# Decoding in place in four slots, separate opening banks, and moved sums in the first two token groups of an attention, gated-layer and expert kernel

## The chip, the cores and the metric

The kernel runs on one core of one Trainium2 chip. The metric is the device time of one execution in microseconds; the median of several runs is given.

## The reference

Three layers follow one another, all in float32. Keys and values are averaged over 8 neighbouring positions, so each of the 8 batches has 72 keys. `w_in` and `w_out` arrive as 64-bit floats.

```python
# q, k, v: (8, 8, 576, 64)
k_p = k.reshape(B, H, 72, 8, D).mean(axis=3);  v_p = likewise
scores = q @ k_p^T / sqrt(D);  attn = softmax(scores);  x = attn @ v_p   # 4608 tokens x 512
h = x @ w_in            # 512 x 2048, float64 in memory
x2 = (h * cos(h)) @ w_out
logits = x2 @ w_gate    # 8 experts, the best one is taken
out = gate_w * (relu(x2 @ w1[e]) @ w2[e])
```

## The kernel before

The 4608 tokens are worked on in 12 groups (g = 0 to 11): 512 tokens, then 256, then 384 each. A group is 16 slots (s = 0 to 15), one for each 128 columns of `w_in`. The order of instructions on every engine is written out by hand; each engine runs its own in that order, and semaphores hold an instruction until what it reads or overwrites is free.

In slot s TensorE (PE) does `mm1(g, s)` into bank HB[s % 2] (L461), then `mm2(g, s - 2)` (L505). The chain between them, in group 0, is: ScalarE (ACT) L479 and L480 (scaled copy and rounded copy), VectorE (DVE) L485, ACT sine L486, DVE product L496, which reads HB[s % 2] and so gives it free for `mm1(s + 2)`, ACT cast L497, GpSimd (POOL) rest L498. L485 reads two tensors in SBUF, L496 one in PSUM.

Group 0 also turns the float64 weights into pairs of float32, in pieces of 128 x 512. Slot s scales the pair of pieces s + 3 on ACT (L600, half before and half behind the sine), does the bit passes of pair s + 2 on DVE, and splits pair s + 1 into high (ACT cast, L612) and low part (POOL, L613), `w_parts`; then `w_load(s + 5)` is issued on SyncE's queue (SP). The bit passes are three for each piece, six a slot: L605 (one tensor in), L606 (two) and L607 (two, the result goes to `u` in SBUF). Their intermediate `b` is a PSUM bank from `rot()`, which in the slots of group 0 hands out banks 5 and 7 in turn:

```python
wl, wh, u, b = self.w[:, :, 0].bitcast(U32), self.w[:, :, 1].bitcast(U32), self.v.bitcast(U32), rot().bitcast(U32)
```

The same two banks take the attention of the next group: `scores(g + 1, i)` (`qk` on PE, L391 to L394, then `soft`: four DVE operations L402, L404 and an exponential L410 on ACT), `norm(i)` (DVE L415 to L417, POOL L418) and `transp(g + 1, i)` (PE L425, copies by ACT L435 and DVE L437). They stand in the list `ex[s]`, which is issued behind the slot's own chain, so on PE they come behind `mm2(s - 2)` and ahead of `mm1(s + 1)`. ACT has the sine in one table and the exponential in another, and loads the table when it changes.

Sums: `pool_k` (L356) and `pool_v` (L378) reduce the keys and values of the next batch on DVE. The raw tiles of batch 1 lie in `kvb`, memory of tags wb8 to wb11, which later holds the converted pieces of `w_out` 8 to 11; so the cast of such a piece waits for the `pool_v` that reads there. Keys are loaded ahead of slot 0, values all four by `early_v` in slot 6.

The opening, ahead of slot 0, does the attention of group 0: four tiles of 128 tokens (`qk`, `soft`, `norm`, `transp`), with runs of `warm` matmuls (L655) between, which give PE something to do. `use(...)` sets the banks that `rot()` hands out, and `warm(n, bank)` writes into the bank named. Then come the bit passes of pairs 0 and 1, `pool_v`, and `pv` (L448 on PE, L452 on ACT, L453 on DVE).

From group 1 on DVE computes the router's logits of the group before, 24 `route_dot` a group (L538, two SBUF tensors in), in numbers for each slot; then `route_sel` (the best expert; L548 to L556) and `route_pos`, which begins with two small matmuls on PE (L569, L570) that read what `route_sel` wrote.

Of the kernel before, what the change touches and what calls it, by code (L numbers as in the profile page):

```python
# [81 lines left out]
def attention_moe_kernel(ctx, tc, qT, kT, vP, w_in, w_out, wg, w1, w2, cst, tri, wgt, out, dbg=None):  # L82
# [25 lines left out]
    def rot():  # L108
        b = rbanks[rot_i[0] % len(rbanks)]
        rot_i[0] += 1  # L110
        return b
# [11 lines left out]
    def w_tmp(s):  # L123
        n_tmp[0] += 1
        return wbp.tile([128, 1024], F32, name=f"tmp{n_tmp[0]}", tag=f"wb{s}")
# [231 lines left out]

    vraw = {}

    def early_v():  # L360
        for c in range(4):
            load_v(1, c)

    def next_k(c):
        if c > 0:
            pool_k(2, c - 1)
# [4 lines left out]
    def load_v(b, c):  # L371
        t = w_tmp(8 + c)[0:KP] if b == 0 else (kvb[c] if b == 1 else raw())[0:KP]
        SP.dma_start(out=t, in_=vP[b, c])
        vraw[b, c] = t
# [8 lines left out]
    def qk(g, i):  # L383
        t0, T = i * TP, BEGIN[g] // TP + i
        b0, b1 = T * TP // S, (T * TP + TP - 1) // S
        sc = [rot(), rot()]
        for pr in range(4):
            for h, r in enumerate((slice(0, 64), slice(64, 128))):
                o = sc[h][:, KP * pr:KP * pr + KP]
                if b0 == b1:  # L390
                    PE.matmul(o, lhsT=qs(g, pr)[r, t0:t0 + TP], rhs=kp[b0 % 2][r, pr], start=True, stop=True)  # L391
                else:
                    PE.matmul(o[0:64], lhsT=qs(g, pr)[r, t0:t0 + 64], rhs=kp[b0 % 2][r, pr], start=True, stop=True)
                    PE.matmul(o[64:128], lhsT=qs(g, pr)[r, t0 + 64:t0 + TP], rhs=kp[b1 % 2][r, pr], start=True, stop=True)  # L394
        return sc
# [74 lines left out]
        DVE.scalar_tensor_tensor(a, r, MAGIC, a, op0=ALU.subtract, op1=ALU.subtract)  # L470
        ACT.activation(a, a, AF.Sin, scale=-TWOPI)  # L471

    def first_slot(s):
        h, a, r = HB[s % 2], tA(0, s % 2), kin[:, 0:W0]
        scales = [p.scale for p in pairs[s + 3]] if s + 3 < NCH else [bool] * 2
        bits = w_bits(s + 2)
        if s > 0:
            w_parts(s + 1)
        ACT.activation(a, h, AF.Identity, scale=INV2PI, bias=consts[:, C_TP + 1:C_TP + 2])  # L479
        ACT.activation(r, a, AF.Identity, bias=consts[:, C_TP + 2:C_TP + 3])  # L480
        if s == 0:
            w_parts(1)
        scales[0]()
        do(bits[0:2])
        DVE.scalar_tensor_tensor(a, r, MAGIC, a, op0=ALU.subtract, op1=ALU.subtract)  # L485
        ACT.activation(a, a, AF.Sin, scale=-TWOPI)  # L486
        scales[1]()
        do(bits[2:4])
        chain_b(0, s)
        do(bits[4:6])  # L490
        w_load(s + 5)

    def chain_b(g, s):
# [93 lines left out]
    class Piece:  # L587
# [11 lines left out]
        def scale(self):  # L599
            ACT.mul(self.w[:, :, 1], self.w[:, :, 1], 2.0 ** -112)  # L600

        def bits(self, u):
            self.v = u
            wl, wh, u, b = self.w[:, :, 0].bitcast(U32), self.w[:, :, 1].bitcast(U32), self.v.bitcast(U32), rot().bitcast(U32)
            return [lambda: DVE.tensor_scalar(b, wh, 3, 0x7FFFFFF8, op0=ALU.logical_shift_left, op1=ALU.bitwise_and),  # L605
                    lambda: DVE.scalar_tensor_tensor(b, wl, 29, b, op0=ALU.logical_shift_right, op1=ALU.bitwise_or),  # L606
                    lambda: DVE.scalar_tensor_tensor(u, wh, 0x80000000, b, op0=ALU.bitwise_and, op1=ALU.bitwise_or)]  # L607
# [30 lines left out]
            for p in pairs[k]:  # L638
                p.scale()

    def w_bits(k):
        if k >= NCH:
            return [bool] * 6
        o = 2 * (k % 3)
        a, b = (p.bits(u) for p, u in zip(pairs[k], us[o:o + 2]))
        return [f for ab in zip(a, b) for f in ab]

    def use(*ids):
        rbanks[:] = [banks[i] for i in ids]
        rot_i[0] = 0  # L650

    def warm(n, bank):

        for i in range(n):
            PE.matmul(banks[bank][:, 384:512], lhsT=ident, rhs=ident, start=True, stop=True)  # L655

    def do(ops):
        for f in ops:
            f()

    def w_parts(k):
        if k < NCH:
            for p in pairs[k]:
                p.parts()
# [23 lines left out]
    u13 = w_tmp(13)  # L688
    us += [u[:, DM * i:DM * i + DM] for u in (u13, ldt[0]) for i in range(2)]
    w_load(2)  # L690
    use(*range(8))
    sc = [qk(0, 0), qk(0, 1)]
    soft(0, sc[0], True)
    pool_v(0, 0)
    soft(1, sc[1], True)
    sc += [qk(0, 2), qk(0, 3)]
    warm(6, 3)
    norm(0, True)
    pool_v(0, 1)
    use(0, 1)  # L700
    transp(0, 0, True)
    warm(4, 7)
    soft(2, sc[2])
    norm(1, True)
    soft(3, sc[3])
    w_scale(0)
    norm(2)
    norm(3)
    use(0, 1)
    bits = w_bits(0)  # L710
    do(bits)
    for i in range(1, 4):
        use(2 * i, 2 * i + 1)
        transp(0, i, True)
        warm((8, 2, 4)[i - 1], (7, 7, 5)[i - 1])
    pool_v(0, 2)
    pool_v(0, 3)
    w_load(3)
    kvb[:] = [w_tmp(8 + i) for i in range(4)]
    for c in range(4):  # L720
        load_k(1, c)
    use(5, 7)
    bits = w_bits(1)
    use(2, 3, 4, 6)
    for c in range(4):
        if c < 2:
            pairs[0][c].parts()
        elif c < 4:
            pairs[1][c - 2].scale()
        pv(0, c)  # L730
        do(bits[0 if c < 2 else c - 2:max(0, c - 1)])
    do(bits[2:6])
    w_load(4)
    w_scale(2)
    ACT.activation(st1[:, 0:1], consts[:, C_TP + 1:C_TP + 2], AF.Sin)
    POOL.tensor_copy(trib, E3[:, 0:256])
    POOL.tensor_copy(run, consts[:, C_OFF:C_OFF + 8])
# [15 lines left out]

    for g in range(NG):
        ex = {s: [] for s in range(NCH)}

        def at(s, f, *a):
            ex[s].append(lambda: f(*a))

        if g + 1 < NG:  # L760
            for i in range(TILES[g + 1]):
                if g == 0:
                    at((6, 10)[i], scores, g + 1, i)
                    at((6, 10)[i], norm, i)
                    at((8, 11)[i], transp, g + 1, i)
                else:
                    o = 1 if g == 1 else 0
                    at(1 + o + 4 * i, scores, g + 1, i)
                    if i == 0 and g > 1:
                        at(1, route_exp)  # L770
                    at(1 + o + 4 * i, norm, i)
                    at(4 + o + 4 * i, transp, g + 1, i)
            if 0 < g < NG - 2:
                at(11 if g == 1 else 10, load_q, g + 2)
            if g == 0:
                at(4, load_q, 1)
                for i in range(2):
                    w = slice(2048 - 2048 * i, 4096 - 2048 * i)
                    at(12 + 2 * i, lambda w=w: SP.dma_start(out=wgb[:, w], in_=wgt[w].unsqueeze(0).to_broadcast([128, 2048])))
                for i in range(3):  # L780
                    at(13 + i, next_k, i)
        dots = {}
        if g > 0:
            last = g == NG - 1
            n = 0
            for s, k in enumerate((0, 3, 4, 3, 4, 3, 4, 3) if last else (0, 2, 1, 3, 3, 2, 1, 3, 3, 2, 1, 3) if g == 1 else (0, 1, 3, 3, 2, 1, 3, 2, 2, 1, 2, 4)):
                dots[s] = list(range(n, n + k))
                n += k
            if last:
                at(1, route_exp)  # L790
                at(8, route_sel, g - 1)
                at(8, route_exp)
                at(9, route_pos)
                at(9, route_gate, g - 1)
                for i in range(3):
                    at(10, route_put, i)
            else:
                at(11 if g == 1 else 12, route_sel, g - 1)
                at(12 if g == 1 else 14, route_pos)
        if g > 1:  # L800
            at(2, route_gate, g - 2)
            for i in range(3):
# [5 lines left out]
                    at((0, 2, 3)[c], load_v, 2, c + 1)  # L808
        for b in range(1, B):
            if g == max(0, b * S // GT - 2):  # L810
                if b == 1:
                    at(6, early_v)
                for c in range(4):
                    if b == 1:
                        at(2 + c, pool_k, b, c)
                        at(7 + c, pool_v, b, c)
                    elif b > 2:
                        at(2 + 2 * c, pool_k, b, c)
                        at(2 * c, load_k, b, c)
                if b == 2:  # L820
                    at(0, next_k, 3)
                    at(1, next_k, 4)
                    at(14, load_v, b, 0)
                if b > 2:
                    for c in range(4):
                        at((7, 10, 12, 14)[c], pool_v, b, c)
                        at((5, 7, 10, 12)[c], load_v, b, c)
        for s in range(NCH):
# [11 lines left out]
                mm2(g, s - 2)  # L840

            if g == 0:
                first_slot(s)
            elif g == NG - 1 and 6 < s < 15:
                c = (s - 7,)
                chain_a(g, s, lambda: split(0, -50, 0, c, False, (0,)))
            else:
                chain_a(g, s)
# [7 lines left out]
            if first_x:  # L856
                E1.append(ep.tile([128, 2048], F32R, name="E1", tag="e1"))
                for i in range(2):
                    tx_parts(XP[i], *unit_x(i))
            todo = dots.get(s, [])  # L860
            if todo:
                route_dot(g - 1, todo.pop(0))
# [363 lines left out]
```

## Time and profile before

| | |
|---|---|
| median of 3 runs | 1481.0 us (1477.67 to 1481.91) |
| profiled execution, own time | 1491.82 us |
| its span | 1490.0 us |
| PE busy | 1423.9 us, 96% of the span |
| DVE / ACT / POOL busy | 878.2 / 735.6 / 448.4 us |
| granted PE clock, mean | 0.983 |

The profiled execution is longer than the median by 10.8 us. Busy time is a sum over the whole span; what holds PE up in a certain slot is read from the waits and the timeline there. A clock of 1.00 is 2.4 GHz, 0.50 is 1.2 GHz.

### The profile page before, as it was taken

To read this page: it belongs to the slowest core of one execution; us is meant where nothing else is said; L and a number is where in the kernel's file an instruction comes from. 1 tells how busy PE (TensorE), PEld (TensorE's weight loads), DVE (VectorE), ACT (ScalarE), POOL (GpSimd) and SP (SyncE) were. 2 spreads that over 40 slices of the span, in tenths; PEclk is the share of its full clock that TensorE was granted. 3 is DMA by queue.
4 is the path that set the end of the run, shared out by engine and by line. 5 is a ranking of instruction groups with operands and counts; after the bars stand their busy time and mean duration, and the time that the engine had idled before them with its cause. 6 is when DMAs were issued, how large, how long until landed. Compare 5 with 4: busy or idle time off the path is not lost. (4 is left out here: it accounts for less than half of the span.)

```text
span 1490.0 us, 23426 instructions
## 1 busy us (share of the span) xinstructions
PE 1423.9 (96%) x8343; PEld 1224.6 (82%) x8343; DVE 878.2 (59%) x1948; ACT 735.6 (49%) x1360; POOL 448.4 (30%) x421
## 2 busy tenths in 40 slices
PE   7878989999999999999999999999999999999998
PEld 5656778888898988888888888888787878899997
DVE  6976677867686867586867585863252142124222
ACT  5866566566565656565656565661131131123111
POOL 2654223233333333232324242432131121113212
PEclk9988999999999999999999999999999999999999
DMA  7552202200121200121200001215565434001110
GB/s 245 189 162 104 67 30 69 62 23 22 40 64 42 62 30 22 37 63 38 69 31 22 22 1 43 94 37 203 212 236 195 151 146 153 31 29 55 50 37 31
DMA packets 42485, 119.96 MB, mean 81 GB/s; under 512 B 6227, under 2 KB 21715, under 8 KB 39520
## 3 DMA queue, kind: packets, MB, share of 16 engines
q1 hardware_dynamic: 34416, 99.17, 19.7%
q0 software_dynamic: 7920, 18.97, 4.0%
q8 instruction: 73, 1.20, 0.3%
q14 instruction: 76, 0.62, 0.2%
HBM read 101.55 MB, written 19.66 MB: 81 GB/s over the span
## 5 line engine op out<-in xcount | busy, mean ns | idle before, releaser
L505 PE MATMUL bank<-wb,GB 128*128 128x512 f32 x1696 | 434.0, 396 | 0.1
L461 PE MATMUL bank<-xh,WI 128*128 128x384 f32 (+2 forms) x1504 | 427.9, 347 | 5.7 <-DVE att L496 3.5
L505 PEld LDWEIGHTS bank<-wb,GB 128*128 128x128 f32 x1696 | 315.2, 188 | 71.1 <-issue 5.3
L461 PEld LDWEIGHTS bank<-xh,WI 128*128 128x128 f32 x1504 | 278.7, 192 | 22.0 <-DVE att L496 4.2
L461 PE MATMUL bank<-xl,WI 128*128 128x384 f32 (+2 forms) x752 | 256.7, 341 | 0.0
L937 PEld LDWEIGHTS bank<-E,wb 128*128 128x128 f32 x1632 | 210.8, 192 | 20.3 <-issue 8.7
L937 PE MATMUL bank<-E,wb 128*128 128x256 f32 x1632 | 216.6, 285 | 4.2 <-DVEq L1142 2.1
L538 DVE SCALAR_TENSOR_TENSOR E<-x2t,wgb 128x512 bf16<-128x512 f32 x264 | 213.1, 807 | 2.1
L946 PE MATMUL bank<-wb,xh 128*128 128x512 f32 x816 | 210.4, 396 | 0.0
L928 ACT ACTIVATE xh<-bank 128x256 fp32r<-128x256 f32 x136 | 52.2, 384 | 297.8 <-PE bank L937 296.1
L929 DVE SCALAR_TENSOR_TENSOR xh<-bank,xh 128x256 fp32r<-128x256 f32 x136 | 57.6, 424 | 218.0 <-ACT xh L928 91.9
L498 POOL TENSOR_TENSOR GB<-E,GB 128x384 fp32r<-128x384 f32 (+1 forms) x88 | 96.4, 1095 | 243.7 <-ACT GB L497 207.7
L498 POOL TENSOR_TENSOR GB<-TA,GB 128x384 fp32r<-128x384 f32 (+1 forms) x88 | 97.7, 1110 | 234.8 <-ACT GB L497 234.8
L946 PEld LDWEIGHTS bank<-wb,xh 128*128 128x128 f32 x816 | 145.5, 189 | 25.4 <-issue 0.2
L461 PEld LDWEIGHTS bank<-xl,WI 128*128 128x128 f32 x752 | 144.4, 192 | 6.5
L199 POOL DMA_INDIRECT E<-x2d,E x44 | 46.0, 1045 | 271.5 <-PE bank L744 258.2
L470 DVE SCALAR_TENSOR_TENSOR TA<-bank,TA 128x384 f32<-128x384 f32 (+1 forms) x88 | 47.4, 539 | 77.0 <-ACT bank L468 75.7
L470 DVE SCALAR_TENSOR_TENSOR E<-bank,E 128x384 f32<-128x384 f32 (+1 forms) x88 | 47.5, 540 | 59.9 <-ACT bank L468 58.8
L497 ACT CAST GB<-E 128x384 fp32r<-128x384 f32 (+2 forms) x96 | 49.3, 513 | 65.4 <-DVE E L496 61.9
L471 ACT ACTIVATE E<-E 128x384 f32<-128x384 f32 (+1 forms) x88 | 45.4, 516 | 68.5 <-DVE E L470 68.3
L467 ACT ACTIVATE TA<-bank,consts 128x384 f32<-128x384 f32 (+1 forms) x88 | 49.6, 564 | 44.4 <-PE bank L461 44.4
L497 ACT CAST GB<-TA 128x384 fp32r<-128x384 f32 (+1 forms) x88 | 44.5, 505 | 53.8 <-DVE TA L496 46.5
(243 smaller groups left out, 1747.9 us busy)
## 6 DMA issues: line engine op xcount, KB each, us to landing
rst<-w SPq DMA_DIRECT2D x12, 2048.0 KB
stg<-w SPq DMA_DIRECT2D x6, 2048.0 KB
x2d<-x2t SPq DMA_DIRECT2D x36, 256.0 KB
QF<-qT SPq DMA_DIRECT2D x10, 768.0 KB
E<-kT SPq DMA_DIRECT2D x24, 288.0 KB
E<-vP SPq DMA_DIRECT2D x24, 288.0 KB
wgb<-w_in SPq DMA_DIRECT2D x11, 512.0 KB
wgb<-w_out SPq DMA_DIRECT2D x11, 512.0 KB
```

The costliest lines, as they stand in the source:

```text
L199: POOL.indirect_dma_start(out=xg[i], out_offset=None, in_=x2d[0:n], in_offset=bass.IndirectOffsetOnAxis(ap=column(u, i)[0], axis=0), bound ...
L461: PE.matmul(o, lhsT=a, rhs=xT(g, k, c), start=n == 0, stop=n == 11)
L467: ACT.activation(a, h, AF.Identity, scale=INV2PI, bias=consts[:, C_TP + 1:C_TP + 2])
L470: DVE.scalar_tensor_tensor(a, r, MAGIC, a, op0=ALU.subtract, op1=ALU.subtract)
L497: ACT.copy(h, a)
L498: POOL.tensor_tensor(l, a, h.bitcast(F32), op=ALU.subtract)
L505: PE.matmul(acc, lhsT=a[:, sl], rhs=w_tile(s)[:, DM * w:DM * w + DM], start=s == 0 and n == 0, stop=s == NCH - 1 and n == 2)
L538: DVE.scalar_tensor_tensor(junk, x2[i], 1.0, wgb[:, DM * e:DM * e + DM], op0=ALU.mult, op1=ALU.mult, accum_out=lgs[:, i, e:e + 1])
L928: ACT.activation(h, o, AF.Relu)
L929: DVE.scalar_tensor_tensor(l, o, 0.0, h.bitcast(F32), op0=ALU.max, op1=ALU.subtract)
L937: PE.matmul(o, lhsT=w_tile(4 * w + s // 2)[:, f], rhs=x[:, c], start=n == 0, stop=n == 11)
L946: PE.matmul(OP[i], lhsT=a[s % 3][:, 128 * i:128 * i + 128], rhs=w_piece(w, s), start=s == 0 and n == 0, stop=s == 7 and n == 2)
```

## The change

The bit passes of slots 6, 8, 9 and 11 use `u` itself for the intermediate, so they take no PSUM bank, and all their operands lie in SBUF. The scores of the second tile move from slot 10 to slot 9. `norm` moves one slot later and stands ahead of L485 (a new list `soon`). Values are loaded one by one behind each `pool_k`, one slot earlier, and `pool_v` goes to slots 5, 7, 8 and 10. In slot 0 the order within the chain changes, and the two scale passes `w_scale(2)` come there from the opening. In the opening the `warm` matmuls get bank 7 for themselves and the other uses other banks. In group 1, dots, `norm`, one key sum, `route_sel` and `route_pos` move to other slots.

```diff
-    def first_slot(s):
+    def first_slot(s, soon):
         h, a, r = HB[s % 2], tA(0, s % 2), kin[:, 0:W0]
-        bits = w_bits(s + 2)
+        bits = w_bits(s + 2, s in (6, 8, 9, 11))
         if s > 0:
             w_parts(s + 1)
         ACT.activation(a, h, AF.Identity, scale=INV2PI, bias=consts[:, C_TP + 1:C_TP + 2])
         ACT.activation(r, a, AF.Identity, bias=consts[:, C_TP + 2:C_TP + 3])
         if s == 0:
+            w_scale(2)
             w_parts(1)
+        else:
+            do(bits[0:2])
         scales[0]()
-        do(bits[0:2])
+        for f in soon:
+            f()
         DVE.scalar_tensor_tensor(a, r, MAGIC, a, op0=ALU.subtract, op1=ALU.subtract)
         ACT.activation(a, a, AF.Sin, scale=-TWOPI)
         scales[1]()
-        do(bits[2:4])
+        do(bits[0:2] if s == 0 else bits[2:4])
         chain_b(0, s)
-        do(bits[4:6])
+        do(bits[2:6] if s == 0 else bits[4:6])
         w_load(s + 5)
...
-        def bits(self, u):
+        def bits(self, u, place):
...
+            b = u if place else rot().bitcast(U32)
...
-    def warm(n, bank):
+    def warm(n):
...
-            PE.matmul(banks[bank][:, 384:512], lhsT=ident, rhs=ident, start=True, stop=True)
+            PE.matmul(banks[7][:, 0:128], lhsT=ident, rhs=ident, start=True, stop=True)
...
-    use(*range(8))
+    use(0, 1, 2, 3, 4, 5)
...
-    sc += [qk(0, 2), qk(0, 3)]
-    warm(6, 3)
+    sc.append(qk(0, 2))
+    warm(4)
+    use(6, 0)
+    sc.append(qk(0, 3))
     norm(0, True)
     pool_v(0, 1)
-    use(0, 1)
+    use(1, 3)
     transp(0, 0, True)
-    warm(4, 7)
+    warm(4)
...
-    use(0, 1)
+    use(2, 3)
     bits = w_bits(0)
     do(bits)
-    for i in range(1, 4):
-        use(2 * i, 2 * i + 1)
-        transp(0, i, True)
-        warm((8, 2, 4)[i - 1], (7, 7, 5)[i - 1])
+    for i, two in enumerate(((1, 4), (5, 1), (6, 0))):
+        use(*two)
+        transp(0, i + 1, True)
+        warm((8, 2, 4)[i])
...
+    kvb_i[0] = -1
...
-    use(5, 7)
+    use(2, 3)
     bits = w_bits(1)
-    use(2, 3, 4, 6)
+    use(4, 5, 1, 6)
...
-    w_scale(2)
...
-                    at((6, 10)[i], scores, g + 1, i)
-                    at((6, 10)[i], norm, i)
+                    at((6, 9)[i], scores, g + 1, i)
+                    soon[(7, 10)[i]].append(lambda i=i: norm(i))
                     at((8, 11)[i], transp, g + 1, i)
...
-                    at(1 + o + 4 * i, norm, i)
+                    if g == 1:
+                        soon[3 + 4 * i].append(lambda i=i: norm(i))
+                    else:
+                        at(1 + 4 * i, norm, i)
...
-                at(4, load_q, 1)
+                at(1, load_q, 1)
...
-  (0, 2, 1, 3, 3, 2, 1, 3, 3, 2, 1, 3) if g == 1
+  (2, 3, 1, 2, 3, 3, 1, 2, 3, 2, 0, 2) if g == 1
...
-                at(11 if g == 1 else 12, route_sel, g - 1)
-                at(12 if g == 1 else 14, route_pos)
+                at(12, route_sel, g - 1)
+                at(14, route_pos)
...
-                if b == 1:
-                    at(6, early_v)
                 for c in range(4):
                     if b == 1:
-                        at(2 + c, pool_k, b, c)
-                        at(7 + c, pool_v, b, c)
+                        at(1 + c, pool_k, b, c)
+                        at(1 + c, load_v, b, c)
+                        at((5, 7, 8, 10)[c], pool_v, b, c)
...
-                    at(1, next_k, 4)
+                    at(3, next_k, 4)
```

## Rows read from the trace of the kernel before

**Rows 1.** Windows: busy us (x instructions) of each engine, PE clock, DMA share, GB/s.

```profile
275.00:1490.00 1215.00, 1188.17 (x7060) 1030.37 (x7059) 673.98 (x1540) 561.99 (x1034) 339.65 (x325) 0.99 0.21 71
```

**Rows 2.** Waits of PE, whole span: us in total, times, longest.

```profile
PE bank L425 <- DVE tmp L607: 6.9, 2, 4.1
PE bank L393 <- DVE E L607: 6.2, 1, 6.2
PE bank L569 <- DVE oh L556: 5.1, 2, 4.2
PE bank L461 <- DVE att L496: 3.5, 1, 3.5
PE bank L391 <- ACT GB L497: 3.4, 1, 3.4
```

**Rows 3.** Windows behind two of these waits, columns as in rows 1.

```profile
80.00:82.00 2.00, 1.91 (x33) 1.55 (x34) 0.87 (x2) 1.23 (x1) 1.27 (x1) 0.50 0.42 120
211.00:216.00 5.00, 4.89 (x24) 4.50 (x24) 1.93 (x9) 2.13 (x5) 0.75 (x1) 0.66 0.00 0
```

**Rows 4.** Timeline of the opening: start, us, engine, instruction, [idle before <-releaser].

```profile
18.72 1.15 POOL L418 TENSOR_TENSOR tmp<-tmp,rss 128x576 f32<-128x576 f32 x1 [1.96 <-DVE rss L417]
...
23.80 0.46 DVE L402 TENSOR_REDUCE mxs<-bank 128x4 f32<-128x288 f32 x1 [4.41 <-PE bank L655]
24.80 2.05 PE L655 MATMUL bank<-consts 128*128 128x128 f32 x16 [0.17 <-DVE tmp L404]
...
28.75 1.07 PE L425 MATMUL bank<-consts,tmp 128*72 128x128 f32 x8
...
34.37 0.51 PE L461 MATMUL bank<-xh,WI 128*128 128x512 f32 x1
```

**Rows 5.** Timeline of DVE, from the product of slot 3 to that of slot 4.

```profile
61.34 0.68 DVE L496 TENSOR_TENSOR E<-bank,E 128x512 f32<-128x512 f32 x1
61.94 1.27 DVE L607 SCALAR_TENSOR_TENSOR E<-tmp,bank 128x512 uint32<-128x512 uint32 x2
...
65.24 0.72 DVE L485 SCALAR_TENSOR_TENSOR att<-E,att 128x512 f32<-128x512 f32 x1 [0.18 <-ACT E L480]
65.89 1.28 DVE L606 SCALAR_TENSOR_TENSOR bank<-wgb,bank 128x512 uint32<-128x512 uint32 x2
67.08 0.68 DVE L496 TENSOR_TENSOR att<-bank,att 128x512 f32<-128x512 f32 x1
```

**Rows 6.** Timeline of DVE and POOL, slots 1 and 4.

```profile
46.91 1.84 DVE L485 SCALAR_TENSOR_TENSOR E<-E,E 128x512 f32<-128x512 f32 x1 [0.89 <-issue]
46.92 1.29 POOL L613 TENSOR_TENSOR wb<-E,wb 128x512 fp32r<-128x512 f32 x1
...
65.37 1.76 POOL L613 TENSOR_TENSOR wb<-E,wb 128x512 fp32r<-128x512 f32 x1
```

**Rows 7.** Timeline of DVE and ACT, slots 6 and 7.

```profile
81.53 0.46 DVE L402 TENSOR_REDUCE mxs<-bank 128x4 f32<-128x288 f32 x1 [1.12 <-PE bank L394]
83.37 0.68 ACT L410 ACTIVATE tmp<-tmp 128x576 f32<-128x576 f32 x1 [2.14 <-DVE tmp L404]
84.09 0.75 DVE L415 TENSOR_REDUCE rss<-tmp 128x8 f32<-128x576 f32 x1 [0.75 <-ACT tmp L410]
...
86.22 0.69 ACT L479 ACTIVATE E<-bank,consts 128x512 f32<-128x512 f32 x1 [1.14 <-PE bank L461]
88.25 1.28 ACT L486 ACT_TABLE_LOAD   x1
...
92.01 1.21 DVE L378 TENSOR_REDUCE E<-tmp 72x128 f32<-72x1024 f32 x1
```

**Rows 8.** Timeline of ACT, start of slot 8.

```profile
93.26 0.62 ACT L612 CAST wb<-x2t 128x512 fp32r<-128x512 f32 x1 [1.10 <-DVE E L378]
```

**Rows 9.** Timeline of PE, first matmuls of slots 13 and 14.

```profile
136.84 0.39 PE L461 MATMUL bank<-xh,WI 128*128 128x512 f32 x1
...
142.43 0.39 PE L461 MATMUL bank<-xh,WI 128*128 128x512 f32 x1
```

More of the change, by code (lines that the diff above doesn't have):

```diff
@@ L358, in attention_moe_kernel @@
     vraw = {}
-    def early_v():
-        for c in range(4):
-            load_v(1, c)
     def next_k(c):
@@ L600, in scale @@
             ACT.mul(self.w[:, :, 1], self.w[:, :, 1], 2.0 ** -112)
-        def bits(self, u):
+        def bits(self, u, place):
             self.v = u
-            wl, wh, u, b = self.w[:, :, 0].bitcast(U32), self.w[:, :, 1].bitcast(U32), self.v.bitcast(U32), rot().bitcast(U32)
+            wl, wh, u = self.w[:, :, 0].bitcast(U32), self.w[:, :, 1].bitcast(U32), self.v.bitcast(U32)
+            b = u if place else rot().bitcast(U32)
             return [lambda: DVE.tensor_scalar(b, wh, 3, 0x7FFFFFF8, op0=ALU.logical_shift_left, op1=ALU.bitwise_and),
@@ L639, in w_scale, with w_bits @@
                 p.scale()
-    def w_bits(k):
+    def w_bits(k, place=False):
         if k >= NCH:
@@ L644, in w_bits @@
         o = 2 * (k % 3)
-        a, b = (p.bits(u) for p, u in zip(pairs[k], us[o:o + 2]))
+        a, b = (p.bits(u, place) for p, u in zip(pairs[k], us[o:o + 2]))
         return [f for ab in zip(a, b) for f in ab]
@@ L727, in attention_moe_kernel @@
             pairs[0][c].parts()
-        elif c < 4:
+        else:
             pairs[1][c - 2].scale()
@@ L755, in attention_moe_kernel @@
         ex = {s: [] for s in range(NCH)}
+        soon = {s: [] for s in range(NCH)}
         def at(s, f, *a):
@@ L770, in attention_moe_kernel @@
                         at(1, route_exp)
-                    at(1 + o + 4 * i, norm, i)
+                    if g == 1:
+                        soon[3 + 4 * i].append(lambda i=i: norm(i))
+                    else:
+                        at(1 + 4 * i, norm, i)
                     at(4 + o + 4 * i, transp, g + 1, i)
@@ L785, in attention_moe_kernel @@
             n = 0
-            for s, k in enumerate((0, 3, 4, 3, 4, 3, 4, 3) if last else (0, 2, 1, 3, 3, 2, 1, 3, 3, 2, 1, 3) if g == 1 else (0, 1, 3, 3, 2, 1, 3, 2, 2, 1, 2, 4)):
+            for s, k in enumerate((0, 3, 4, 3, 4, 3, 4, 3) if last else (2, 3, 1, 2, 3, 3, 1, 2, 3, 2, 0, 2) if g == 1 else (0, 1, 3, 3, 2, 1, 3, 2, 2, 1, 2, 4)):
                 dots[s] = list(range(n, n + k))
@@ L842, in attention_moe_kernel @@
             if g == 0:
-                first_slot(s)
+                first_slot(s, soon[s])
             elif g == NG - 1 and 6 < s < 15:
@@ L859, in attention_moe_kernel @@
                     tx_parts(XP[i], *unit_x(i))
+            if g == 1:
+                for f in soon[s]:
+                    f()
             todo = dots.get(s, [])
```

## The prediction

> **What bounds the kernel now.** I read the waits of PE first, then the windows, then the timeline of each engine around the longest waits. From 275 us to the end PE is busy 1188 of 1215 us at a clock of 0.99 [rows 1]. The change touches nothing there, so what is won or lost ahead of 275 us reaches the end one to one. Ahead of it the reader is to see five kinds of wait [rows 2]: PE waits 6.9 us in two pieces and 6.2 us in one for L607, the last bit pass of a slot; 3.4 us at the scores of slot 10, where the view names ACT but the banks were held by bit passes too; 3.5 us for L496 of slot 0; and 4.2 us in one piece for `route_sel`. All but the 3.5 and the 4.2 come from one thing: scores and transposes take their banks from the same two as the bit passes of the slot just issued, and PE, in order, stands until DVE has done that slot. Behind such a wait the clock was 0.50 for a stretch (80 to 82) and 0.66 over 211 to 216 [rows 3], so each costs more than its own length: 5 us at 0.66 are 1.7 us lost.
>
> Between attention slots DVE and ACT set the pace. From L496 of slot 3 to that of slot 4 are 5.74 us [rows 5]. L485 starts 3.3 us behind the end of L496 (61.94, where the next pass starts) and waited only 0.18 us for ACT; then come 0.65 for L485, 1.2 for two L606 and 0.6 for L496. PE needs 5.6 us for a slot (136.84 to 142.43) [rows 9], so such slots keep it nearly full, and every addition on that chain makes PE wait.
>
> **The opening.** DVE stands 4.41 us ahead of the second half of tile 3's scores, until `warm` matmuls in the same bank are done [rows 4]. With bank 7 for `warm` alone this wait goes, and the first transposes no longer stand behind 12 matmuls that themselves wait for a bank. What is late next? The `norm` of tile 1 on POOL ends at 18.72 + 1.15 = 19.87 whatever the banks do; the transposes of tile 1 take 1.07 (as those at 28.75) and end at 20.95. From the matmuls behind them (24.80) to the first `mm1` (34.37) PE took 9.57 us, of which some 0.1 was waiting for things that are now early. The same list of work follows now, so `mm1(0)` starts at 20.95 + 9.45 = 30.4: **4.0 us earlier**. DVE's bit passes move by more than that (its 4.41 us are gone ahead of them), so PE is the later of the two. Bounds: nothing, if the first weights land only just in time, which no row shows; 4.4 us, all of DVE's wait.
>
> Slot 0: L485 no longer follows two bit passes, but its sine now stands on ACT behind two scale passes more. The one takes off about what the other adds, so I count the 3.5 us wait as it is, and its bounds are nothing gained and 1 us gained. At the product of slot 5 the lead is still 4.0: between slots 1 and 5 the chain of 5.74 us rules, and the key sums, moved one slot earlier, lie beside it as they do now: in slot 4 DVE had such a sum and still waited 0.18 us for ACT [rows 5]. The moved loads of values and queries stand on SP's queue behind `w_load` of their slot, with nothing behind them but the `w_load` of the next, a slot later.
>
> **Slots 6 to 12.** I follow L496 to L496. A slot on DVE is: two L607 (1.2), what `ex` adds, two L605 (1.2), L485 (0.65), two L606 (1.2), L496 (0.6) [rows 5].
>
> *The four slots in place.* L606 and L607 get a second SBUF operand, and L605 its output in SBUF; the trace before has no such pass. The nearest row is L485, also with two SBUF operands: 0.72 us against 0.64 for a pass with PSUM, with the same 0.65 from start to start [rows 5]. I take the same length. But rows 6 show a price: L485 of slot 1 took 1.84 us, and its POOL neighbour, which started 0.01 us later, the usual 1.29; in slot 4 L485 was there first, and the POOL operation took 1.76. DVE and POOL pass each other one whole operation at a time when DVE reads two SBUF tensors. The Trainium skill has this in SBUF — State Buffer, section Who interferes with whom: a VectorE instruction with two SBUF inputs and a GpSimd instruction that reads SBUF shut each other out for a whole instruction; it speaks against the change, and the rows agree. The page VectorE: DVE Perf Modes, section Mode 2×_2P, adds that a single-input operation within SBUF may go at two results a cycle, so L605 in place could be some 0.3 us shorter each, an estimate that no row here bears out.
>
> POOL has three operations a slot. The third is due at 65.37, 3.4 us behind the end of L496, and lasts 1.29, so it ends 4.7 us behind it [rows 5, 6]. DVE comes to L485 at 1.2 + 1.2 (`pool_v` [rows 7]) + 1.2 = 3.6, while POOL is at work. I let POOL keep its turn once: L485 at 4.7, the passes behind it free, and the period is 4.7 + 0.65 + 1.2 + 0.6 = 7.15 for slots 6, 8 and 11. Slot 9 has a copy of 0.6 more on DVE, which pushes POOL a little too: 7.4. If DVE never loses, L485 starts at 3.6 (4.2 in slot 9): 6.05 and 6.65, together 4.1 us less. If two more POOL operations go first in every one of the four, 4 x 2 x 1.29 = 10.3 us more.
>
> *The two slots behind scores (7 and 10).* From the end of L496: 1.2 for L607, 1.84 for the four DVE operations of the softmax (81.53 to 83.37), then ACT's chain: from the exponential to L479 1.71 us (86.22 less its wait of 1.14 for PE, less 83.37), to the table 2.03, the table 1.28; then 0.66 for the sine and 0.6 for L496 [rows 7]: 9.35 us. `norm` now stands inside that chain ahead of L485, where DVE waits for ACT anyway: it is due 1.2 behind the softmax, after the L605 pair, and done about 1.1 later (84.09 with its 0.75 and two short ones), while ACT gives L485 free 1.71 + 1.4 behind the exponential. If the cover were gone it would cost 1.1 us twice.
>
> *Slot 12* has a copy of 0.6 and ACT another: 6.2. The second cast of slots 8, 9 and 10, which waited for `pool_v` (1.10 in slot 8 [rows 8]), no longer does, since its `pool_v` is now a slot or more earlier; slot 11 still does, hidden behind POOL's third operation.
>
> Sum: 3 x 7.15 + 7.4 + 2 x 9.35 + 6.2 = 53.75 us from L496 of slot 5 to that of slot 12. `mm1(14)` starts 0.65 us behind it: 54.4. Before, L496 of slot 5 was at 67.08 + 5.74 = 72.8, and `mm1(14)` at 142.43 [rows 5, 9]: 69.6. **Gain 15.2 us.** PE fits in: its seven slots need 7 x 5.6 = 39.2, the transposes 1.07 twice [rows 4], and the scores an estimated 2 twice, from their sixteen small matmuls: some 45. It still waits, but the scores of slot 6 wait for the passes of slot 5 only (some 1 us against 6.2), and the transposes of slots 8 and 11 for those of 7 and 10 (some 3 us each against 4.1 and 2.8). Those of slot 11 may leave the clock low for one `mm1`; that stands close to the end of the chain, and I take off **1.3 us** for it (bounds 0 and 2.6: from nothing to 24 matmuls at the lower level, half of it hidden).
>
> **Group 1.** With `route_sel` in slot 12 and `route_pos` two slots behind it, PE's matmuls come when DVE has long been done: the 4.2 us go, and the 1.7 us of low clock [rows 2, 3]. Dots in slot 0 stand ahead of L496 there and read rows that ACT has just copied; I charge 0.6 us for them, and with 24 dots as before nothing else. The key sum that moves from slot 1 to 3 only leaves more time for its load. **Gain 5.3 us.**
>
> **Sum.** 4.0 + 15.2 - 1.3 + 5.3 = 23.2 us. The profiled execution's 1491.8 becomes 1468.6; the median of the runs is 10.8 below the profiled one, and I take the gain from it whole: 1481.0 - 23.2 = **1457.8**.
>
> **The rivals.**
>
> *POOL goes first.* In the four slots DVE loses two more turns: 10.3 us less gain, 1468. For it: in slot 1 POOL's next operation went ahead of a DVE instruction that came at the same moment [rows 6]. Against: POOL has only three operations a slot, and two have mostly run by the time the in-place pairs come.
>
> *The opening gives nothing.* The first weights or their scaling are what is late next: 1481.0 - 19.2 = 1462. For it: no row shows when they land. Against: DVE's passes there waited for nothing once the 4.41 us were over.
>
> *Attention waits as before.* The banks are still held, by the slot before, and DVE is later in it; if each of the four places waits as long as before, only opening and group 1 are left, 9.3 us, and something of slots 8 to 10: 1470. For it: slots 7 and 10 stay at 9.35 us, so L607 there comes late. Against: the chain above.
>
> *Slower: the clock stays low.* PE would be busy some 45 of 54 us in slots 6 to 12. If it were at 0.50 throughout, a slot would need nearly twice its 5.6 us, some 10.5, which is 2.8 more than the mean period of 7.7: 20 us over seven slots, and 4.9 for each slot behind. It decides from slot 13 on, where the 23 us are used up; up to the end of slot 15 it comes to some 34 us: 1492. Against: in rows 3 the level of 0.50 ended while PE worked on, and 211 to 216 was mixed, with 4.9 of 5 us busy.
>
> **How the numbers follow.** The sum has 0.62; POOL first 0.15; no gain in the opening 0.11; attention waits as before 0.07; low clock 0.04; and 0.01 is left for no change. A measurement here can tell some 0.3%, or 4.4 us. So faster 0.95, same 0.01, slower 0.04. The likeliest case alone reaches from 1452 (DVE never loses, no low clock) to 1463. For 8 in 10 the range takes in the first two rivals: 1451 to 1469.
>
> **What would show it.** `mm1(0)` near 30.4; L402 of tile 3 without a wait; the scores of slot 6 waiting about 1 us; L485 in slots 6, 8, 9 and 11 up to 1.7 us long; L496 of slots 7 and 10 some 9.3 us behind the one before; `mm1(14)` near 123; no wait at L569 in group 1. It is wrong if in-place passes are themselves longer than 0.7 us, if they queue behind POOL one by one, or if `mm1` runs at half speed through whole slots.

## The result, and the profile after

The changed kernel takes 1461.0 us (median of 4 runs, 1459.35 to 1462.11) and the kernel before, beside it, 1480.6 (1477.67 to 1481.91): a ratio of 0.987, with a 95% interval of 0.985 to 0.989. That is 19.6 us less. Forecast were 1457.8 us, 23.2 less, with a range of 1451 to 1469.

The two profiled executions stand further apart than that: spans of 1490.0 and 1457.5, or 32.5 us. So I compare by place: the first matmul, the first `mm1` of slot 14, the first scores in group 1 and the first in group 2 stood at 34.37, 142.43 [rows 4, 9], 169.51 and 232.46 before. The timeline of PE shows the last two before, and then all four after, with the transposes of slot 11 among them:

```profile
169.51 1.43 PE L391 MATMUL bank<-E,QF 64*128 64x72 f32 x16 [1.95 <-DMA QF<-qT]
...
232.46 1.11 PE L391 MATMUL bank<-E,QF 64*128 64x72 f32 x16
```

```profile
30.77 0.50 PE L457 MATMUL bank<-xh,WI 128*128 128x512 f32 x1
...
112.41 1.89 PE L421 MATMUL bank<-consts,tmp 128*72 128x128 f32 x8 [3.92 <-DVE x2t L608]
...
126.87 0.39 PE L457 MATMUL bank<-xh,WI 128*128 128x512 f32 x1
...
155.36 0.89 PE L387 MATMUL bank<-E,QF 64*128 64x72 f32 x12 [2.13 <-DMA QF<-qT]
...
212.57 1.11 PE L387 MATMUL bank<-E,QF 64*128 64x72 f32 x16
```

The lead grows from 3.6 to 15.6, sinks to 14.2 and is 19.9 in group 2. All of the measured 19.6 us is there. The other 12.6 us of the span difference arise behind it, in the expert layer, which the change does not touch. Two rows by line, of before and then of after, show from when to when one group of six small matmuls ran, and what they waited for in all:

```profile
L1022 PE MATMUL bank<-consts,xl x6: 273/421/476, 1054.3 to 1212.1; 128*128 128x128 f32 x6
its engine sat idle before it (us, times) until:
  ACT xl L1019: 8.0, 3
```

```profile
L1031 PE MATMUL bank<-consts,xl x6: 272/300/328, 1032.5 to 1181.4; 128*128 128x128 f32 x6
its engine sat idle before it (us, times) until:
  ACT xl L1028: 1.5, 3
```

Before it took 157.8 us, after 148.9: 8.9 of the 12.6. The rest lies in two pieces of some 1.9 us, ahead of these matmuls and behind them. The wait of three times 2.7 us in place of 0.5 goes with the chip and not with the kernel (last section). The 10.8 us by which the profiled execution of before stood above the other runs are of the same size; that they have this cause is likely, and not shown.

The waits of PE, longest first, without those of the expert layer, answer to [rows 2]:

```profile
PE bank L421 <- DVE x2t L608: 8.0, 2, 4.1
...
PE bank L457 <- DVE att L496: 2.7, 1, 2.7
...
PE bank L389 <- DVE tmp L608: 0.8, 2, 0.5
```

The 6.2 us at the scores of slot 6 are down to 0.8 in two pieces, the 3.4 at the scores of slot 10 and the 4.2 for `route_sel` are gone. The transposes, L421, still wait 8.0 us: some 3 us each were forecast, and 4.07 and 3.92 came. The windows show that the rest is as full as it was [rows 1], and the clock behind the second of these waits:

```profile
255.11:1457.50 1202.39, 1181.28 (x7060) 1027.68 (x7059) 675.93 (x1540) 562.07 (x1034) 339.46 (x325) 1.00 0.21 72
...
113.00:116.00 3.00, 3.00 (x12) 2.47 (x11) 1.66 (x3) 1.94 (x4) 3.00 (x3) 0.50 0.82 295
116.00:118.70 2.70, 2.70 (x10) 2.12 (x9) 2.68 (x3) 1.62 (x3) 1.04 (x1) 0.70 0.17 67
```

What the forecast got wrong in size is in the timeline of DVE and POOL in slot 6, from the product of slot 5 to that of slot 6 (start, us, instruction; beside [rows 5, 6]):

```profile
69.05 0.68 DVE L496 TENSOR_TENSOR E<-bank,E 128x512 f32<-128x512 f32 x1
69.65 1.27 DVE L608 SCALAR_TENSOR_TENSOR tmp<-wgb,bank 128x512 uint32<-128x512 uint32 x2
70.84 1.20 DVE L374 TENSOR_REDUCE E<-tmp 72x128 f32<-72x1024 f32 x1
71.97 0.74 DVE L606 TENSOR_SCALAR E<-tmp 128x512 uint32<-128x512 uint32 x2
72.95 1.47 DVE L485 SCALAR_TENSOR_TENSOR att<-E,att 128x512 f32<-128x512 f32 x1 [0.23 <-ACT E L476]
74.35 2.39 DVE L607 SCALAR_TENSOR_TENSOR E<-tmp,E 128x512 uint32<-128x512 uint32 x2
76.66 0.68 DVE L496 TENSOR_TENSOR att<-bank,att 128x512 f32<-128x512 f32 x1
...
71.81 2.06 POOL L614 TENSOR_TENSOR WI<-tmp,WI 128x512 fp32r<-128x512 f32 x1
73.84 1.75 POOL L614 TENSOR_TENSOR wb<-tmp,wb 128x512 fp32r<-128x512 f32 x1
```

From 71.97 on the two engines take turns. DVE's L606 pair runs until 72.71, and POOL's first L614, which has its usual 1.28 us to do, takes 2.06. DVE's L485 starts at 72.95 and ends at 74.42, 0.55 behind that POOL operation. POOL's second L614 then ends at 75.59, and DVE's L607 pair, 1.28 us of work, ends 1.15 behind that. The period is 7.61 us; 7.15 were forecast. Not every pass takes turns: the sum, L374, with one input in SBUF, ran its usual 1.20 us while POOL's L498, from 70.58 on, ran its usual 1.28.

L485 and the L607 pair have two inputs in SBUF. For them this is the rule named ahead of the result (the Trainium skill, SBUF — State Buffer, section Who interferes with whom), and the trace agrees with it for two turns in a row, not for one. The L606 pair has only one input, and POOL still lost 0.78 us beside it. In place that pair took 0.74 us, where a pair with PSUM takes 1.28. The Trainium skill, VectorE: DVE Perf Modes, section Mode 2×_2P, has two results a cycle for one input within SBUF; the prediction's estimate from it was some 0.3 us less for each pass, and the trace agrees, with some 0.27 less.

### The profile page after: what moved, and what is told of

Its sections match the earlier page's. It is cut to its first block, busy times and chain, and to the rows that moved or that the text cites. A ratio compares the mean times of both kernels' runs of the same rounds, so it can differ in the third digit from the quotient of the medians.

```text
span 1457.5 us, 23415 instructions
## 1 busy us (share of the span) xinstructions
PE 1410.9 (97%) x8339; PEld 1214.8 (83%) x8339; DVE 884.8 (61%) x1948; ACT 734.5 (50%) x1360; POOL 454.0 (31%) x421
## 5 line engine op out<-in xcount | busy, mean ns | idle before, releaser
L457 PEld LDWEIGHTS bank<-xh,WI 128*128 128x128 f32 x1504 | 275.3, 189 | 22.7 <-DVE E L496 5.3
L498 POOL TENSOR_TENSOR GB<-E,GB 128x384 fp32r<-128x384 f32 (+1 forms) x88 | 96.5, 1097 | 236.7 <-ACT GB L497 201.6
L498 POOL TENSOR_TENSOR GB<-TA,GB 128x384 fp32r<-128x384 f32 (+1 forms) x88 | 97.4, 1107 | 229.5 <-ACT GB L497 229.5
```

Source lines behind the costliest of these rows:

```text
L457: PE.matmul(o, lhsT=a, rhs=xT(g, k, c), start=n == 0, stop=n == 11)
L498: POOL.tensor_tensor(l, a, h.bitcast(F32), op=ALU.subtract)
```

## The experiments

Times were compared with the kernel before on the same chip. On three further chips that kernel took 1488.8, 1479.1 and 1489.6 us, so only differences are used. A second run of the changed kernel tells how far a single trace can be trusted:

> The changed kernel once more, as the measure for the two others on the same chip: 19.6 us under the kernel before by every theory, within the scatter of a few us.

It took 1473.0 us against 1489.6, a ratio of 0.990 (0.988 to 0.991): 16.6 us less. From the first `mm1` to the scores in group 2 it took 183.9 us, where the first execution took 181.8 (212.57 less 30.77) and the kernel before 198.1. I call this stretch "the way to group 2". Two traces of one kernel differ by 2 us in it, so less than that is not told apart below.

Of these 2 us 1.2 are a single turn, in slot 2, whose period was 5.71 us in the first execution and 6.88 in the second. L485 and a POOL operation start 0.02 us apart there; in the first execution DVE had the turn, in the second POOL:

```profile
49.96 0.69 DVE L485 SCALAR_TENSOR_TENSOR att<-E,att 128x512 f32<-128x512 f32 x1 [0.17 <-ACT E L476]
49.98 1.84 POOL L614 TENSOR_TENSOR wb<-x2t,wb 128x512 fp32r<-128x512 f32 x1
```

```profile
50.08 1.86 DVE L485 SCALAR_TENSOR_TENSOR att<-E,att 128x512 f32<-128x512 f32 x1 [0.18 <-ACT E L476]
50.10 1.30 POOL L614 TENSOR_TENSOR wb<-x2t,wb 128x512 fp32r<-128x512 f32 x1
```

So where the two come within some 0.02 us of each other, one and the same kernel goes either way, and a forecast turn by turn is open there by one turn.

**The opening alone** (bank 7 for `warm`, the other banks dealt out anew and the scores of tile 3 behind the first `warm` matmuls, in the kernel before):

```diff
...
-            PE.matmul(banks[bank][:, 384:512], lhsT=ident, rhs=ident, start=True, stop=True)
+            PE.matmul(banks[7][:, 0:128], lhsT=ident, rhs=ident, start=True, stop=True)
...
-    use(2, 3, 4, 6)
+    use(4, 5, 1, 6)
```

> The kernel before with the opening's banks alone changed (warm matmuls in a bank of their own, other uses apart); slots and group 1 as before. Theory (the wait for the warm matmuls' bank held up the whole opening): the first matmul of slot 0 starts near 30.8 in place of 34.4, and the time is 3 to 4 us under the kernel before, about 1477 us. Rival (the later stalls of group 0 swallow the lead, because VectorE's chain and not PE sets them): the lead is gone by slot 14, and the time is within 1 us of 1480.6.

1477.0 against 1479.1, a ratio of 0.9988 (0.9977 to 0.9999): 2.1 us less. The first `mm1` is at 30.60, 3.8 us earlier, and the product of slot 5 still 3.6 earlier (69.26 against 72.84). By slot 12 the lead is 2.3 (135.19 against 137.52): slots 7, 9 and 11 took 0.8, 0.1 and 0.3 us longer than before. In slot 7 the loss is PE's: the low clock behind the scores of slot 6 lasted longer. From 3.0 to 4.8 us behind the start of that slot's matmuls the clock was still 0.50, where it was 0.94 in the kernel before (second row), and ACT waited 1.92 us for them in place of 1.14:

```profile
81.06:82.86 1.80, 1.80 (x5) 1.37 (x5) 1.73 (x5) 0.46 (x1) 0.99 (x1) 0.50 0.76 193
...
84.62:86.42 1.80, 1.80 (x8) 1.41 (x8) 1.73 (x5) 0.66 (x2) 0.99 (x1) 0.94 0.77 187
```

So by itself the opening keeps about half of what it gains at its own place, between theory and rival; the interval takes in 0.1 to 3.4 us.

**In place undone:**

```diff
-        bits = w_bits(s + 2, s in (6, 8, 9, 11))
+        bits = w_bits(s + 2, False)
```

> The changed kernel with the bit passes of all slots in PSUM again; everything else stays changed. Theory (in-place passes free the banks): scores of slots 6 and 9 and transposes of slots 8 and 11 wait on PE for the last bit pass of their own slot again, 3 to 6 us each; the first matmul of slot 14 comes some 11 us later than in the changed kernel (126.9), and the time is about 1472 us. Rival (the port shared with GpSimd takes back what the free banks give, and the gain of the slots came from the moved sums and norm): within 2 us of 1461.

1480.2 against 1488.8, 0.994 (0.991 to 0.997): 8.6 us less than before, where the whole change brought 16.6 to 19.6. The way to group 2 is 192.0 us, 8 to 10 longer than in the changed kernel. From the first `mm1` to that of slot 14 it is 106.2 us, 9 to 10 longer (96.1 and 97.2), where some 11 were expected; the rival is out. The wait of the scores of slot 6 is back among the waits of PE:

```profile
PE bank L421 <- DVE tmp L608: 7.1, 2, 4.1
PE bank L389 <- DVE E L608: 6.4, 1, 6.4
```

That of the transposes (L421) was there in the changed kernel too, 8.0 us against 7.1 here: this wait is not what the change takes away. Slots 7, 9, 10 and 12 took 2.1 to 2.9 us longer without the in-place passes, and slots 6, 8 and 11 0.8 to 1.7 us less, which is what in-place passes cost there.

**Group 1 as before** (its dots, `norm`, `route_sel`, `route_pos` and one key sum where they were):

```diff
...
-                at(12, route_sel, g - 1)
+                at(11 if g == 1 else 12, route_sel, g - 1)
...
-                    at(3, next_k, 4)
+                    at(1, next_k, 4)
```

> The changed kernel with the dots, norm, key sum, best-expert step and its matmuls of group 1 in their old slots. Theory (what was won in group 1 is one wait of PE for the best-expert step and the low clock behind it): that wait of about 4 us is back, and the time is 5 to 6 us more, about 1466.5 us. Rival (VectorE is as full either way, so the wait only moves to another place in group 1 or 2): within 2 us of 1461.

1476.5 against 1488.8, 0.991 (0.989 to 0.993): 12.3 us less, so these moves are worth 4 to 7. The wait is back whole, and the way to group 2 is 188.8 us, 5 to 7 longer:

```profile
PE bank L569 <- DVE oh L556: 5.0, 2, 4.2
```

**In place in slots 2 to 5 as well**, where no attention needs a bank:

```diff
-        bits = w_bits(s + 2, s in (6, 8, 9, 11))
+        bits = w_bits(s + 2, s in (2, 3, 4, 5, 6, 8, 9, 11))
```

> The changed kernel with slots 2 to 5 in place as well, where no attention stands that could gain by it. Theory (an in-place slot costs the turns that VectorE and GpSimd take at the shared port): each of the four goes from 5.75 us to about 7.6, so the product of slot 5 comes some 7.5 us later than at 69.05, and the time is about 1468.5 us. Rival (slots 6, 8, 9 and 11 are long because of the sums and copies in them, not because of the port): under 1 us a slot, so 1461 to 1464 us.

1477.8 against 1488.8, 0.993 (0.991 to 0.995): 11.0 us less, so 6 to 9 slower than the changed kernel. The four slots took 30.0 us in place of 23.0 (products at 45.80 and 75.81; 46.05 and 69.05 in the changed kernel). This is what in-place passes cost where they save no wait. In slots 3 to 5 a period was 7.6 us, the same as in slots 6 and 8. DVE again takes its turns behind POOL:

```profile
55.51 2.30 DVE L606 TENSOR_SCALAR E<-tmp 128x512 uint32<-128x512 uint32 x2
57.73 1.77 DVE L485 SCALAR_TENSOR_TENSOR E<-E,E 128x512 f32<-128x512 f32 x1
```

**POOL reads nothing beside the in-place passes.** The low parts of the weights in these four slots are filled with zeros, so this part of the computation is left out.

```diff
...
+            if blank:
+                POOL.memset(lo.bitcast(F32), 0.0)
+            else:
+                POOL.tensor_tensor(lo, v, hi.bitcast(F32), op=ALU.subtract)
...
```

> The changed kernel, but in slots 6, 8, 9 and 11 GpSimd writes zeros for the low parts of the weights in place of subtracting; so the low parts of weight pairs 7, 9, 10 and 12 are left out of the result. Theory (turns at the shared port): the rounding subtraction and the second bit pass of these slots run at 0.7 us each without standing behind GpSimd, the four slots shrink from 7.6 to 8.2 us to about 6.0 to 6.6, and the time is 4 to 6 us less than the changed kernel, 1455 to 1457 us. Rival (in-place passes are slow by themselves, or ScalarE's chain sets these slots): within 1.5 us of 1461.

1466.3 against 1488.8, 0.986 (0.984 to 0.987): 22.5 us less. The periods of slots 6, 8, 9 and 11 are 6.08, 6.09, 6.31 and 6.85 us; the first two are the 6.05 that the prediction gave for a DVE that never loses. That is close in part by luck, since its L606 pair was counted at 1.2 us and took 1.43, as slot 6 shows:

```profile
72.13 1.43 DVE L606 TENSOR_SCALAR E<-tmp 128x512 uint32<-128x512 uint32 x2
73.47 0.68 DVE L485 SCALAR_TENSOR_TENSOR att<-E,att 128x512 f32<-128x512 f32 x1
74.08 1.28 DVE L607 SCALAR_TENSOR_TENSOR E<-tmp,E 128x512 uint32<-128x512 uint32 x2
```

POOL's two writes, 0.53 us each, are over by 72.95, and L485 and the L607 pair, alone then, have their usual length. The L606 pair has not: beside the writes it took 1.43 and not 0.74, so the fast pass within SBUF was held up by operations of POOL that read nothing. So the run shows what the two turns behind POOL's subtractions cost together: at least 1.5 us in slots 6 and 8 (7.61 less 6.08).

**The second low part later.** Computed in full, but POOL's second subtraction of these four slots is issued behind the product:

```diff
+        later = []
+        if s in (6, 8, 9, 11):
+            pairs[s + 1][0].parts()
+            pairs[s + 1][1].parts(later)
...
         chain_b(0, s)
+        do(later)
...
```

> The changed kernel, but in slots 6, 8, 9 and 11 the second low part of the weights is subtracted by GpSimd behind the slot's own rest, one operation later, when the in-place passes ahead of the product are over. Theory (in these slots the shared port is full: VectorE's operations on it and GpSimd's three add up to the whole slot): slots 6 and 8 shrink from 7.6 us by about 1, slot 9 stays, slot 11 shrinks a little, and the time is 1.5 to 3 us under the changed kernel. Rival (order on GpSimd changes nothing, its operations come one slot later at the same cost): within 1 us of the changed kernel.

1467.7 against 1489.6, 0.986 (0.984 to 0.987): 21.9 us less, and 5.3 us under the changed kernel on this chip (1473.0), whose range of runs it does not touch (1466.8 to 1468.5 against 1471.5 to 1477.3). That is more than the 1.5 to 3 us expected. Slots 6 and 8 took 6.50 us and slot 11 6.85, together 3.1 us less; what the other 2 us are is open. Slot 6 shows that only the first turn is left:

```profile
73.32 0.75 DVE L611 TENSOR_SCALAR E<-tmp 128x512 uint32<-128x512 uint32 x2
74.30 1.47 DVE L489 SCALAR_TENSOR_TENSOR att<-E,att 128x512 f32<-128x512 f32 x1 [0.23 <-ACT E L480]
75.69 1.28 DVE L612 SCALAR_TENSOR_TENSOR E<-tmp,E 128x512 uint32<-128x512 uint32 x2
...
73.16 2.07 POOL L619 TENSOR_TENSOR WI<-tmp,WI 128x512 fp32r<-128x512 f32 x1
...
79.89 1.30 POOL L619 TENSOR_TENSOR wb<-tmp,wb 128x512 fp32r<-128x512 f32 x1
```

Slot 9 kept 8.21 us, and it supports the same reading. The operation put off from slot 8 lies in it, so POOL has two subtractions there as before, and the L612 pair still loses its turn:

```profile
95.63 2.43 POOL L619 TENSOR_TENSOR wb<-x2t,wb 128x512 fp32r<-128x512 f32 x1
98.02 1.74 POOL L619 TENSOR_TENSOR WI<-tmp,WI 128x512 fp32r<-128x512 f32 x1
98.53 2.38 DVE L612 SCALAR_TENSOR_TENSOR E<-tmp,E 128x512 uint32<-128x512 uint32 x2
```

**In place in slots 7 and 10 too**, so that the transposes of slots 8 and 11 need no bank of theirs:

```diff
-        bits = w_bits(s + 2, s in (6, 8, 9, 11))
+        bits = w_bits(s + 2, 5 < s < 12)
```

> The changed kernel with slots 7 and 10 in place as well, so that the transposes of slots 8 and 11 need no bank of theirs. Theory (VectorE's chain sets slots 6 to 12, and PE's two waits of 4 us at the transposes only show it): the waits shrink to about 2.5 us, where norm is due, but the two slots get longer by up to 1.5 us each at the shared port; the time is the same or up to 3 us more, 1461 to 1464 us. Rival (these waits of PE cost their length): 3 to 4 us less, about 1457.5 us.

1463.5 against 1479.1, 0.989 (0.987 to 0.992): 15.5 us less, no better than the changed kernel, and some 3 us short of two runs on the same chip that are not told from it (18.6 and 18.3, below). The wait for L608 is gone, and another stands in its place, for `norm` on POOL:

```profile
PE bank L421 <- POOL tmp L414: 3.2, 2, 2.4
```

The scores of slot 9 also wait 2.92 us now, for a copy on ACT (0.17 in the changed kernel, for one on DVE). Slots 7 and 10 took 10.06 and 10.15 us, 0.8 to 0.9 more. So the 8.0 us at the transposes are no price of the banks: PE is ahead of the softmax and waits for it in one form or another.

**Three moves undone, one at a time:** `norm` back in slots 6 and 9; the sums of the values and their loads back where they were; slot 0 in its old order.

```diff
-                    soon[(7, 10)[i]].append(lambda i=i: norm(i))
+                    at((6, 9)[i], norm, i)
```

> The changed kernel with norm of group 0 directly behind its scores, in slots 6 and 9, as it stood before. Theory (one slot later it lies in time in which VectorE waits for ScalarE): VectorE then waits for the exponential with the bit passes of the next slot queued behind norm; 0.5 to 1.5 us more for each, so 1462 to 1464 us. Rival (it costs nothing either way): within 1 us of 1461.

```diff
-                        at(1 + c, load_v, b, c)
-                        at((5, 7, 8, 10)[c], pool_v, b, c)
+                        at(6, load_v, b, c)
+                        at(7 + c, pool_v, b, c)
```

> The changed kernel with the four loads of values in slot 6 and their sums in slots 7 to 10, as before. Theory (the second weight cast of slots 8, 9 and 10 stands on ScalarE until the sum has read the memory that it writes): ScalarE waits 1.1 us in each of these slots again, of which a part lies on the chain; 1 to 3 us more, 1462 to 1464 us. Rival (these slots are set by VectorE and the port, so ScalarE has room): within 1 us of 1461.

```diff
...
-        do(bits[0:2] if s == 0 else bits[2:4])
+        do(bits[2:4])
         chain_b(0, s)
-        do(bits[2:6] if s == 0 else bits[4:6])
+        do(bits[4:6])
...
```

> The changed kernel with the order of slot 0 as before and the two scale passes back in the opening. Theory (what slot 0 wins it gives back in slot 1, where the four bit passes that it pushed behind the product make the next casts late): the product of slot 0 comes some 0.8 us later, those of slots 2 to 5 within 0.4 us, and the time is within 1 us of the changed kernel. Rival (the chain's lead in slot 0 stays): 1 us more or above.

They took 18.6, 18.3 and 18.2 us less than before, with ratios of 0.988 (0.985 to 0.990), 0.988 (0.986 to 0.990) and 0.988 (0.986 to 0.989). The way to group 2 was 183.3, 184.3 and 183.0 us. None is told from the changed kernel: each of the three moves is worth less than some 2.5 us here, alone. The traces say more of the first two: the periods of slots 6 to 12 add up to 56.95 and 57.11 us there and to 56.97 in the changed kernel, so in these slots `norm` and the values gain nothing. The 1 to 3 us more that the theory expected of each did not come.

## Why the prediction was right, and where its sizes were off

The mechanism held: in-place passes free the banks, the opening and group 1 lose their waits, and POOL takes part of the gain back. The sizes did not all hold. By place, the lead is 3.8 us at the product of slot 5, another 11.8 up to `mm1` of slot 14, 1.4 lost up to the scores of group 1, and 5.7 in group 1: 19.9. The forecast was 4.0, 13.9 (15.2 less 1.3), nothing and 5.3.

**The opening** came as forecast: `mm1(0)` at 30.77 for 30.4, and the second half of tile 3's scores is no longer waited for. What was late next was PE's own list of work, not the first weights. That the time fits so well is partly luck. The matmuls behind the transposes of tile 1 were to start at 20.95 and start at 22.22, since PE was still busy with `warm` matmuls when `norm` was done. From there the list took 8.55 us and not 9.45. Of the 9.57 before, 0.1 was taken for waiting; one wait for `norm` on POOL (L418) alone was 0.34.

```profile
22.22 1.95 PE L656 MATMUL bank<-consts 128*128 128x128 f32 x16
```

**Slot 0.** The wait for L496 is 2.75 for 3.5 us. But slot 1 took longer, and at slot 2 nothing is left of it against the old order (20.99 us from the first `mm1` to the product of slot 2, 21.36 in the old order, less than two traces differ). It was counted at nothing, and is.

**Slots 6 to 12: the step that failed** is "I let POOL keep its turn once: L485 at 4.7, the passes behind it free". The seven periods were forecast as 7.15, 9.35, 7.15, 7.4, 9.35, 7.15 and 6.2, and measured as 7.61, 9.22, 7.61, 8.20, 9.29, 7.74 and 7.30: together 56.97 for 53.75. POOL had two subtractions to make, and each pushed a DVE pass: L485 took up to 1.69 us, as foreseen, and then the L607 pair 2.39 for 1.28, which was not. That second turn is 1.1 us in each of slots 6, 8 and 9. The prediction let L485 wait for POOL's third operation, which was to end 4.7 us behind the end of L496. In the trace it waited for the second, which the L606 pair had pushed back and which ended 4.2 us behind it (73.87 less 69.65); that is 0.5 us better than forecast. The third was then still to come, and it is the one that the L607 pair lost to. With the second turn moved, slots 6 and 8 took 6.50, under the forecast; with POOL's subtractions left out 6.08. The rival "POOL goes first" had the right mechanism. It charged two turns more in every slot, and one came, in three of the four. By the prediction's own signs this part was wrong: passes did "queue behind POOL one by one" there, and `mm1(14)` came at 126.87 and not near 123.

Slots 6, 8 and 9 have 1.7 of the 3.2 us over the forecast. Slots 11 and 12 have as much again.

In slot 11 the cause is another. Its second cast on ACT still waited 1.11 us for `pool_v`, and that was not hidden behind POOL, as "hidden behind POOL's third operation" had it. L485 waited for ACT first, and for POOL behind that:

```profile
116.02 1.58 DVE L485 SCALAR_TENSOR_TENSOR E<-E,E 128x512 f32<-128x512 f32 x1 [1.36 <-ACT E L476]
...
123.30 1.60 DVE L485 SCALAR_TENSOR_TENSOR att<-E,att 128x512 f32<-128x512 f32 x1 [0.90 <-ACT E L476]
```

The second row is slot 12, forecast at 6.2 with a copy on each engine added. There ACT's chain let L485 wait 0.90 us, and POOL's subtraction, which ended at 124.35, stretched it to 1.60: the slot came out 1.1 us over its forecast.

**The low clock** was there: 0.50 from 113 to 116, the lower of its two levels, after PE had stood 3.92 us. The 1.3 us taken off for it were too much. PE worked from 112.41 on without a wait, and `mm1` of slot 14 started at 126.87, while the bank that it needs came free with the end of the product of slot 12 at 126.62. So it cost 0.25 us at most. The rival "slower" falls with that: by 120 us PE was at full speed, and had caught up. That the stretch missed its forecast by 2.1 us (11.8 for 13.9) and not by 3.4 (11.8 for 15.2) is luck: the slots were counted too short, and the clock too dear.

**Between slot 14 and group 1** 1.4 us were lost, which no step had. The trace goes some way here. Before, PE was the late one at `mm1` of slot 14: it stood 4.9 us behind the product of slot 12 (142.43 less 137.52), now 0.85. So PE now comes to the end of group 0 early: its second group of `pv` matmuls waits 0.65 us for DVE (L449), where the kernel before had no wait. A part of the lead that `mm1` of slot 14 shows was PE's, not DVE's. From the first group of `pv` to the second 1.04 us were lost (5.12 for 4.08), this wait among them; ahead of that stretch and behind it 0.2 us each. What the other 0.4 in the stretch are is open.

**Group 1** gave 5.7 us for 5.3, and the old order takes it back. **The attention waits** went as the chain had it: 0.8 us at the scores of slot 6, and some 4 at each of the transposes, 1 more than forecast, because slots 7 and 10 kept their 9.2 to 9.3 us. The rival "Attention waits as before" was right on the transposes (8.0 us, 6.9 before) and wrong on the scores, whose 6.2 and 3.4 us went to 0.8 and 0.2. It was wrong on the time, since 11.8 us were won with the waits of the transposes still there; the run with slots 7 and 10 in place shows that they do not cost their length.

## What to carry to other kernels

When a pass moves from PSUM to SBUF to free a bank, count the operations of VectorE and GpSimd in the stretch and add the two up wherever they take turns. Here that was every VectorE pass with two inputs in SBUF and the fast one-input pass within SBUF, against GpSimd's subtractions; the sums did not take turns. Each further operation of GpSimd there can be a further turn lost, not one loss for the stretch. Then look whether the GpSimd operation must stand there at all; here the turn came back by issuing it a few instructions later. Take in-place passes only in slots where a bank is waited for; in the others they cost 1.8 us each (7.0 us over four slots).

Measure a lead at a place on the engine that sets the pace there. A lead of the engine that is merely ahead is partly waited away later.

## What the runs showed that was not expected

The same kernel takes some 10 us more on some chips, and the place of more than half of it can be seen: three times in the expert layer ACT starts L1028 some 2.2 us late, on nothing that its engines record. On the chips where the kernel before took 1488.8 and 1489.6 us, PE's wait there was 7.9 to 8.0 us in every trace, whatever the kernel. On the chip with 1479.1 it was 1.5 in all four traces. The timeline of ACT shows it in one and the same kernel, the changed one, first on the first chip and then on another:

```profile
1032.03 0.38 ACT L1028 ACTIVATE xl<-bank 128x256 f32<-128x256 f32 x1 [3.98 <-PE bank L1027]
```

```profile
1036.26 0.38 ACT L1028 ACTIVATE xl<-bank 128x256 f32<-128x256 f32 x1 [6.09 <-remote]
```

From the first of these six matmuls to the last took 148.9 us in the first case and 155.0 in the second. With the kernel before it was 157.8 on one chip, and 148.2 on the chip with 1479.1 for that kernel with the new opening (1050.5 to 1198.7). What ACT waits for there was not tried.
